# Sigmoid attention and a token/channel mixer on one core: the first group's attention and token mixing in another order

## The chip, the core and the metric

The kernel runs on one core of a Trainium2 chip. Its engines are TensorE (PE; its weight loads are shown as PEld), VectorE (DVE), ScalarE (ACT), GpSimd (POOL) and SyncE (SP). POOL issues the loads from HBM, SP the transposing copies and the stores. The metric is the device time of one execution in microseconds (us), lower is better.

## The reference

For 8 batches, 12 heads, 448 tokens and 64 elements a head, with float32 in HBM:

```python
scores = scale * q @ k.T - log(S)
attn = sigmoid(scores)
x = (attn @ v), heads side by side          # (8, 448, 768)
h = max(x.T @ w_tok1, 0) @ w_tok2           # mixes tokens: 448 -> 256 -> 448
u = x + h.T
out = u + max(u @ w_ch1, 0) @ w_ch2         # mixes channels: 768 -> 1536 -> 768
```

## The kernel before, in words

Matrices are float16 in SBUF, sums float32 in PSUM. Two batches make a group, so there are four groups of 128 rows by 7 token blocks (`J`). A group has six head pairs (`NP`), and a pair has seven score rounds. The order of the instructions on each engine is the order of the program text: nothing is rescheduled.

The steps, with their lines: `load` (L79) brings k, q and v of a pair through POOL. `turn` (L100) transposes k and q of a pair, for the first eight pairs with TensorE (14 small matmuls each, `tk` and `tq`) and a copy out of PSUM, later with a rearranging copy on VectorE and a transposing copy on SP. `scores` (L142) does four matmuls into two banks of PSUM and one sigmoid on ScalarE. `values` (L165) does 28 matmuls over the seven rounds of a pair and copies the result to `xT`, on VectorE for the first group and on ScalarE for the others. `back` (L187) transposes it into `x_nat`. `tok1` (L209) and `tok2` (L226) mix the tokens, with a maximum and a sum after them; the sum is kept as float32 (`u`) and as float16 (`u16`). `uturn` (L293) transposes u16 into `uT` for the channel mixing. `ch1` (L323) and `ch2` (L339) mix the channels, with a maximum and a sum on VectorE.

PSUM has eight banks. Six make three double buffers (`pair_bank`, L63), which scores, values, tok1 and most of tok2 take in turn. Two are single buffers (`bank`, L66), for the transposes, narrow tok2, ch1 and ch2. A matmul into a buffer waits until the engine that read the buffer's last content is done.

`first_attention` (L377) does the first group's attention alone, with no channel mixing to fill gaps. Its `extra` list hangs work behind rounds: the turns of k and q apart, back, and token mixing in three column thirds of 256. Two thirds run inside the attention: tok1 as two stretches of 14 matmuls, then for each of the seven token blocks a tok2, a sum, a cast, two transposes and a copy. The last third follows after the last values (`tok2_late`, L259, which writes u16 first and u afterwards). Before it stands the turn of the second pair of the next group, with ScalarE copying.

`phase` (L427) then does the channel mixing of a group. Between its units, ch1 in 12 steps for four token blocks and 12 for three, then ch2 in 14, stand the next group's score rounds in "visits" of three. A visit may also hold the values of a pair. Each unit has a planned cost, and visits are spread evenly over these costs: 15 visits. After that the next group's tok1, tok2 and uturn stand between ch2 units. The last group has a phase with no attention in it.

The lines that set the visits:

```python
order = [(i, j) for i in range(NP) for j in range(J)]
visits = [order[n : n + 3] for n in range(0, len(order), 3)] + [[]]
for i in range(NP):
    visits[(J * i + J - 1) // 3 + 1].insert(2, (i, None))
step = sum(t for t, _ in units[:n_att]) / len(visits)
```

Of the kernel before, what the change touches and what calls it, by code (L numbers as in the profile page):

```python
# [9 lines left out]
FP16 = mybir.dt.float16  # L10
# [9 lines left out]
def kernel(  # L20
# [26 lines left out]
    JA = 4  # L47
    att_scale = 1.0 / math.sqrt(E)
# [30 lines left out]
    def load(n):  # L79
        g, i = divmod(n, NP)  # L80
        for what, src in (("k", k), ("q", q), ("v", v)):
            t = pa.tile(
                [128, 2, J, E],
                FP16,
                tag="v" if what == "v" else "kq",
                bufs=7 if what == "v" else 8,
                name=f"{what}_{g}_{i}",
            )
            for b in range(2):
                nc.gpsimd.dma_start(  # L90
                    out=t[64 * b : 64 * b + 64, :, :, :],
                    in_=src[2 * g + b, 2 * i : 2 * i + 2].rearrange(
                        "h (p j) e -> p h j e", j=J
                    ),
                )
            heads[(n, what)] = t
# [3 lines left out]
    def turn(n, whats=("k", "q"), eng=nc.vector):  # L100
# [3 lines left out]
        for what in whats:  # L104
# [21 lines left out]
            if eng is nc.vector:  # L126
                eng.tensor_copy(out=t[:, :, :, :], in_=ps[:, :, :, :])  # L127
            else:
                eng.activation(out=t[:, :, :, :], in_=ps[:, :, :, :], func=COPYF)  # L129
        if "q" in whats:  # L130
            load_to(n + 3)

    class Group:
# [31 lines left out]
        def values(self, i):  # L165
# [16 lines left out]
            if self.first:  # L182
                nc.vector.tensor_copy(out=dst, in_=src)
            else:
                nc.scalar.activation(out=dst, in_=src, func=COPYF)
# [23 lines left out]
        def tok1(self, tcb, c0, c1, eng):  # L209
            ps = pair_bank(f"k1_{self.g}_{tcb}_{c0}")  # L210
            for j in range(J):
                for b in range(2):
                    nc.tensor.matmul(  # L213
                        out=ps[:, b, 0 : c1 - c0],
                        lhsT=w_tok1_t[64 * b : 64 * b + 64, j, 128 * tcb : 128 * tcb + 128],
                        rhs=self.x_nat[64 * b : 64 * b + 64, j, c0:c1],
                        start=(j == 0),
                        stop=(j == J - 1),
                    )
            dst, src = self.h1T[:, :, tcb, c0:c1], ps[:, :, 0 : c1 - c0]  # L220
            if eng is nc.vector:
                eng.tensor_scalar(out=dst, in0=src, scalar1=0.0, scalar2=None, op0=MAX)
            else:
                eng.activation(out=dst, in_=src, func=RELU)  # L224

        def tok2(self, j, c0, c1, eng):  # L226
            u, u16 = self.us[j], self.u16s[j]
            if c1 - c0 > 512:
                ps = pair_bank(f"yn_{self.g}_{j}_{c0}")
                w = (c1 - c0) // 2  # L230
                dst = [ps[:, 0, 0:w], ps[:, 1, 0:w]]
                y = ps[:, :, 0:w]
            else:
                w = c1 - c0
                ps = bank(f"yn_{self.g}_{j}_{c0}", [128, w])
                dst = [ps[:, :]]
                y = ps.rearrange("p (n w) -> p n w", n=1)
            for m, d in enumerate(dst):
                for tcb in range(2):
                    for b in range(2):  # L240
                        nc.tensor.matmul(  # L241
                            out=d[64 * b : 64 * b + 64, :],
                            lhsT=w_tok2_n[:, tcb, j, :],
                            rhs=self.h1T[:, b, tcb, c0 + w * m : c0 + w * m + w],
                            start=(tcb == 0),
                            stop=(tcb == 1),
                        )
            nc.vector.tensor_tensor(
                out=u[:, c0:c1].rearrange("p (n w) -> p n w", w=w),
                in0=self.x_nat[:, j, c0:c1].rearrange("p (n w) -> p n w", w=w),  # L250
                in1=y,
                op=ADD,
            )
            if eng is nc.scalar:
                eng.activation(out=u16[:, c0:c1], in_=u[:, c0:c1], func=COPYF)
            else:
                eng.tensor_copy(out=u16[:, c0:c1], in_=u[:, c0:c1])

        def tok2_late(self, js, c0, c1):  # L259

            w = c1 - c0
            name = f"yl_{self.g}_{js[0]}"
            ps = pair_bank(name) if len(js) > 1 else bank(name, [128, 1, w])
            for m, j in enumerate(js):
                for tcb in range(2):
                    for b in range(2):
                        nc.tensor.matmul(
                            out=ps[64 * b : 64 * b + 64, m, 0:w],
                            lhsT=w_tok2_n[:, tcb, j, :],
                            rhs=self.h1T[:, b, tcb, c0:c1],  # L270
                            start=(tcb == 0),
                            stop=(tcb == 1),
                        )
            for m, j in enumerate(js):
                nc.vector.tensor_tensor(
                    out=self.u16s[j][:, c0:c1],
                    in0=self.x_nat[:, j, c0:c1],
# [294 lines left out]
```

## Time and profile before

| what | value |
|---|---|
| median of three runs | 385.68 us (384.07 to 385.81) |
| the profiled execution's own time | 384.07 us |
| its span, first to last instruction | 382.3 us |
| TensorE busy | 360.2 us, 94% of the span |
| VectorE busy | 169.7 us, 44% |
| ScalarE busy | 174.2 us, 46% |
| GpSimd busy | 93.1 us, 24% |
| share of the chain that ended last: PE, DVE, ACT | 89%, 4%, 3% |
| granted TensorE clock | 0.999 |

The page gives an engine's busy time as an average over the whole span. A busy PE there is one that has a matmul in flight, so that it can be full and still lose time where shapes change. The timeline gives for each group of instructions the start, the duration, the engine, the line, the operation and its tiles (written <- read), the shape and the number of instructions; in brackets stands the idle time before it and what ended it. Tiles are named after their step: `qk_g_i_j` a score round, `xa` values, `xb` back, `k_` tok1, `yn` and `yl` tok2, `ut` the transposes of u, and `c_0_3_0` is a ch1 (four blocks) of the first group. The name of a weight tile shows digits left out (`w_tok_t`).

### The profile page before, as it was taken

The numbers are of one execution on the slowest core, as the hardware profiler recorded it, in microseconds if no ns is written. First come the engines' busy times: TensorE is split into PE (matmuls) and PEld (weight loads), VectorE is DVE, ScalarE is ACT, GpSimd is POOL, SyncE is SP. The second block draws the span as 40 slices with busy tenths as digits, with TensorE's granted clock in tenths as the row PEclk, the third lists the DMA queues.
The fourth block names the chain that finished last, engine by engine and source line by source line (L and its number), as shares of the span: only waits on it lengthen the run. The fifth ranks groups of instructions, "written<-read, shape, count | busy, mean of one in ns | idle before, by whom it ended". The sixth has DMA issues, their size and how long they took to land.

```text
span 382.3 us, 8078 instructions
## 1 busy us (share of the span) xinstructions
PE 360.2 (94%) x3404; PEld 189.4 (50%) x3404; DVE 169.7 (44%) x312; ACT 174.2 (46%) x208; POOL 93.1 (24%) x159
## 2 busy tenths in 40 slices
PE   2888987999999999999999999999999999999995
PEld 1444545444555555444555555445555555456663
DVE  1257685553332139544432149444412158555221
ACT  1895752568776510467766410568676210000000
POOL 9888181645154000055153000000000000000000
PEclk9999999999999999999999999999999999999999
DMA  7999999999999936399999927333422327100232
GB/s 102 188 185 172 203 177 201 162 163 146 146 174 134 224 132 155 89 140 123 162 171 172 214 99 165 87 73 74 89 69 74 91 83 158 47 0 0 84 123 84
DMA packets 92372, 49.07 MB, mean 128 GB/s; under 512 B 66096, under 2 KB 88624, under 8 KB 92336
## 3 DMA queue, kind: packets, MB, share of 16 engines
q0 software_dynamic: 25104, 21.93, 40.9%
q1 hardware_dynamic: 67232, 26.62, 36.8%
q8 instruction: 27, 0.44, 0.5%
q14 instruction: 9, 0.07, 0.1%
HBM read 43.84 MB, written 11.01 MB: 143 GB/s over the span
## 4 chain that ended last, share of the span: by engine, by line
PE 89%; DVE 4%; ACT 3%; DMA 1%; issue 1%; POOL 1%; POOLq 0%; ACTq 0%
DMA q_0_78<-in_q_dram 1%; PE c_2_3_1_4494 L343 1%; PE c_2_3_0_4448 L343 1%; PE c_2_2_0_4350 L343 1%; PE c_2_0_1_4232 L343 1%; PE c_1_3_1_3406 L343 1%; PE c_1_3_0_3360 L343 1%; PE c_1_2_0_3262 L343 1%; PE c_1_1_0_3163 L343 1%; PE c_0_3_0_2211 L343 1%; PE c_0_2_1_2148 L343 1%; PE c_0_2_0_2113 L343 1%; PE c_0_1_0_2014 L343 1%; PE c_2_6_1_4697 L343 1%; PE c_2_6_0_4671 L343 1%
## 5 line engine op out<-in xcount | busy, mean ns | idle before, releaser
L326 PEld LDWEIGHTS <-w_ch_t 128*128 128x128 f16 x576 | 53.9, 98 | 58.8 <-issue 12.1
L343 PEld LDWEIGHTS <-h2aT_2475 128*128 128x128 f16 x168 | 15.5, 98 | 13.1 <-issue 3.6
L343 PEld LDWEIGHTS <-h2aT_3624 128*128 128x128 f16 x168 | 15.5, 98 | 13.1 <-issue 3.6
L343 PEld LDWEIGHTS <-h2aT_1316 128*128 128x128 f16 x168 | 15.5, 98 | 13.1 <-issue 3.6
L343 PEld LDWEIGHTS <-h2aT_4712 128*128 128x128 f16 x168 | 16.4, 98 | 10.9
L241 PEld LDWEIGHTS <-w_tok_n 128*64 128x64 f16 x224 | 11.6, 109 | 11.2 <-issue 6.9
L213 PEld LDWEIGHTS <-w_tok_t 64*128 64x128 f16 x252 | 11.5, 94 | 8.8 <-issue 3.0
L90 POOL DMA_DIRECT2D k_0_2644<-in_k_dram x2 | 1.2, 604 | 37.0 <-DVE qp_2535 L110 37.0
L157 ACT ACTIVATE attn_0_0_2494<-qk_0_0_2493 128x896 f16<-128x896 f32 x1 | 0.9, 917 | 17.4 <-PE qk_0_0_2493 L150 17.4
L157 ACT ACTIVATE attn_0_0_3643<-qk_0_0_3642 128x896 f16<-128x896 f32 x1 | 0.9, 917 | 17.4 <-PE qk_0_0_3642 L150 17.4
L121 PE MATMUL tk_133<-ident,k_0_75 128*64 128x128 f16 x14 | 1.0, 312 | 5.2 <-DMA k_0_75<-in_k_dram 5.2
L157 ACT ACTIVATE attn_0_0_167<-qk_0_0_166 128x896 f16<-128x896 f32 x1 | 0.9, 917 | 8.2 <-PE qk_0_0_166 L150 8.2
L127 DVE COPY kT_132<-tk_133 128x896 f16<-128x896 f16 x1 | 0.6, 625 | 6.2 <-PE tk_133 L121 6.2
L121 PEld LDWEIGHTS <-k_0_75 128*64 128x64 f16 x14 | 0.7, 166 | 5.2 <-DMA k_0_75<-in_k_dram 5.2
L90 POOL DMA_DIRECT2D k_3_1923<-in_k_dram x2 | 1.2, 604 | 8.3 <-DVE kp_1804 L110 8.3
L90 POOL DMA_DIRECT2D k_3_3072<-in_k_dram x2 | 1.2, 602 | 8.3 <-DVE kp_2953 L110 8.3
L224 ACT ACTIVATE h1T_2195<-k_1_0_384_2286 128x768 f16<-128x768 f32 x1 | 0.8, 811 | 4.4 <-PE k_1_0_384_2286 L213 4.4
L224 ACT ACTIVATE h1T_4432<-k_3_0_384_4523 128x768 f16<-128x768 f32 x1 | 0.8, 811 | 4.4 <-PE k_3_0_384_4523 L213 4.4
L224 ACT ACTIVATE h1T_3344<-k_2_0_384_3435 128x768 f16<-128x768 f32 x1 | 0.8, 810 | 4.4 <-PE k_2_0_384_3435 L213 4.4
L90 POOL DMA_DIRECT2D k_2_860<-in_k_dram x2 | 1.2, 591 | 6.4 <-PE xb_3_883 L196 3.4
L90 POOL DMA_DIRECT2D k_4_1217<-in_k_dram x2 | 1.2, 590 | 6.4 <-DMA w_ch_t<-in_moe_w_ch_dram 6.4
L129 ACT ACTIVATE kT_1174<-tk_1175 128x896 f16<-128x896 f16 x1 | 0.9, 917 | 3.9 <-PE tk_1175 L121 3.9
(1246 smaller groups left out, 931.2 us busy)
## 6 DMA issues: line engine op xcount, KB each, us to landing
w_ch_t<-in_moe_w_ch_dram POOLq DMA_DIRECT2D x6, 768.0 KB, 12.6
w_tok_t<-in_moe_w_tok_dram POOLq DMA_DIRECT2D x2, 224.0 KB, 6.0
out_dram<-u_0_118 SPq DMA_DIRECT2D x1, 384.0 KB, 8.0
out_dram<-u_1_120 SPq DMA_DIRECT2D x1, 384.0 KB, 6.3
out_dram<-u_2_122 SPq DMA_DIRECT2D x1, 384.0 KB, 4.2
out_dram<-u_3_124 SPq DMA_DIRECT2D x1, 384.0 KB, 2.3
out_dram<-u_4_126 SPq DMA_DIRECT2D x1, 384.0 KB, 3.4
out_dram<-u_5_128 SPq DMA_DIRECT2D x1, 384.0 KB, 2.8
```

Of the source, the lines that this page charges most:

```text
L90: nc.gpsimd.dma_start(out=t[64 * b : 64 * b + 64, :, :, :], in_=src[2 * g + b, 2 * i : 2 * i + 2].rearrange("h (p j) e -> p h j e", j=J),)
L121: nc.tensor.transpose(out=ps[64 * h : 64 * h + 64, j, :, :], in_=raw[:, h, j, :], identity=ident[:, :],)
L127: eng.tensor_copy(out=t[:, :, :, :], in_=ps[:, :, :, :])
L129: eng.activation(out=t[:, :, :, :], in_=ps[:, :, :, :], func=COPYF)
L157: nc.scalar.activation(out=at[:, :, :], in_=ps[:, :, 0:S], func=SIGMOID, bias=att_bias, scale=att_scale,)
L213: nc.tensor.matmul(out=ps[:, b, 0 : c1 - c0], lhsT=w_tok1_t[64 * b : 64 * b + 64, j, 128 * tcb : 128 * tcb + 128], rhs=self.x_nat[64 * b : ...
L224: eng.activation(out=dst, in_=src, func=RELU)
L241: nc.tensor.matmul(out=d[64 * b : 64 * b + 64, :], lhsT=w_tok2_n[:, tcb, j, :], rhs=self.h1T[:, b, tcb, c0 + w * m : c0 + w * m + w], star ...
L326: nc.tensor.matmul(out=ps[:, :, :], lhsT=w_ch1_t[:, db, 128 * cb : 128 * cb + 128], rhs=self.uT[:, db, j0:j1, :], start=(db == 0), stop=(d ...
L343: nc.tensor.matmul(out=ps[:, :], lhsT=self.h2aT[:, cb, j, :], rhs=w_ch2_t[:, cb, c], start=(cb == 0), stop=(cb == NCB - 1),)
```

## The change

The first group's attention is written anew, and some helpers with it. Part by part:

- Loads: v of the first two pairs is loaded behind k and q of both. `turn` always does k and q together and always copies on VectorE.
- Order in a pair i of `first_attention`: two score rounds, the turn of pair i+1, a round, the values of pair i-1, two rounds, back of pair i-1, two rounds, tok1 of pair i-1. Before, the turn of k stood after round 1, that of q after round 3, back after round 5, and tok1 only in pairs 2 and 4.
- tok1 of the first group goes by head pair: 128 columns, both halves of the 256 hidden tokens in one double buffer, 28 matmuls of 128 columns, one maximum on VectorE of 4 x 128.
- tok2 goes by column half (384 columns) in a double buffer. The first half of blocks 0, 1 and 2 runs inside pairs 4 and 5, that of 3 to 6 after the last values. The second half runs late; in a late tok2 of two blocks the second block gets x_nat by an identity matmul into PSUM, so that ScalarE can copy the sum out with no second operand.
- The last values of the first group are copied by ScalarE.
- uturn of two blocks and a half at a time: six transposes and a copy.
- The second half of tok2 of blocks 4 to 6, the transposes of these blocks and the turn of the second pair of the next group stand in the first phase as units of their own, between the first five ch1.
- Visits: the list of rounds with the values counted as rounds (after round 2 of the next pair) is cut in threes, 16 visits, and one more holds the last values. In the first phase the plan starts 6 us late (`ATT_LATE`).

tok1 and tok2 of the other groups have the same matmuls and copies as before.

```diff
+    ATT_LATE = 6.0
...
     def load(n):
...
+        for what, src in (("k", k), ("q", q), ("v", v)):
+            if what == "v" and n < 2:
+                continue
+            load_one(n, what, src)
+        if n == 1:
+            load_one(0, "v", v)
+            load_one(1, "v", v)
...
-            if self.first:
+            if self.first and i < NP - 1:
                 nc.vector.tensor_copy(out=dst, in_=src)
...
+        def tok1(self, c0, c1, tcbs=(0, 1)):
+            w = c1 - c0
+            ps = pair_bank(f"k1_{self.g}_{tcbs[0]}_{c0}")
+            for m, tcb in enumerate(tcbs):
+                for j in range(J):
+                    for b in range(2):
+                        nc.tensor.matmul(
+                            out=ps[:, b, w * m : w * m + w],
...
+        def tok2(self, js, h0=0, h1=2, late=False):
+            ps = pair_bank(f"yn_{self.g}_{js[0]}_{h0}")
+            parts = [(j, half) for j in js for half in range(h0, h1)]
+            for m, (j, half) in enumerate(parts):
+                by_array = late and m == 1
+                if by_array:
+                    nc.tensor.matmul(
+                        out=ps[:, m, 0:DH],
+                        lhsT=ident[:, :],
+                        rhs=self.x_nat[:, j, DH * half : DH * half + DH],
+                        start=True,
+                        stop=False,
+                    )
...
+                def add(dst, x=x, y=y, by_array=late and m == 1):
+                    if by_array:
+                        nc.scalar.activation(out=dst, in_=y, func=COPYF)
+                    else:
+                        nc.vector.tensor_tensor(out=dst, in0=x, in1=y, op=ADD)
+                if late:
+                    add(u16)
+                    steps.append(lambda add=add, u=u: add(u))
+                else:
+                    add(u)
+                    nc.vector.tensor_copy(out=u16, in_=u)
...
     def first_attention(grp):
...
+        early = {(4, 5): (0,), (5, 1): (1,), (5, 5): (2,)}
+        for i in range(NP):
+            for j in range(J):
+                grp.scores(i, j)
+                if j == (1 if i > 0 else 3):
+                    turn(i + 1)
+                elif j == 2 and i > 0:
+                    grp.values(i - 1)
+                elif j == 4 and i > 0:
+                    grp.back(i - 1)
+                elif j == 6 and i > 0:
+                    grp.tok1(128 * i - 128, 128 * i)
+                if (i, j) in early:
+                    grp.tok2(early[(i, j)], 0, 1)
+                if (i, j) == (2, 5):
+                    load_ch1()
+                if (i, j) == (3, 3):
+                    permute_tok2()
+                if (i, j) == (5, 2):
+                    load_ch2()
         grp.values(NP - 1)
+        grp.tok2((3, 4), 0, 1)
         grp.back(NP - 1)
+        grp.uturn((0, 1), 0, 1, nc.vector)
+        grp.tok1(D - 128, D)
+        grp.uturn((2, 3), 0, 1, nc.vector)
+        late = [grp.tok2((0, 1), 1, 2, True), grp.tok2((2, 3), 1, 2, True)]
+        grp.uturn((0, 1), 1, 2, nc.vector)
+        grp.uturn((2, 3), 1, 2)
+        grp.tok2((5, 6), 0, 1)
+        for f in late:
+            f()
...
         for cb in range(NCB):
+            add(1.3, grp.ch1, cb, 0, JA, nc.scalar if grp.first and cb < 3 else nc.vector)
+            if grp.first and cb == 0:
+                add(0.7, grp.tok2, (4, 5), 1, 2)
+            if grp.first and cb == 1:
+                add(0.4, grp.tok2, (6,), 1, 2)
+                add(0.4, grp.uturn, (4, 5), 0, 1)
+            if grp.first and cb == 2:
+                add(0.4, grp.uturn, (4, 5), 1, 2)
+            if grp.first and cb == 3:
+                add(0.4, grp.uturn, (6,))
+            if grp.first and cb == 4:
+                add(1.0, turn, NP + 1)
...
-        order = [(i, j) for i in range(NP) for j in range(J)]
-        visits = [order[n : n + 3] for n in range(0, len(order), 3)] + [[]]
-        for i in range(NP):
-            visits[(J * i + J - 1) // 3 + 1].insert(2, (i, None))
-        step = sum(t for t, _ in units[:n_att]) / len(visits)
+        visits = [rounds[n : n + 3] for n in range(0, len(rounds), 3)]
+        visits.append([(NP - 1, None)])
+        at = -ATT_LATE if grp.first else 0.0
+        step = (at + sum(t for t, _ in units[:n_att])) / len(visits)
```

## The prediction

> **What bounds the kernel now.** I read four views, in this order: the page's 40 slices, the table of stretches, the timeline by engine, the order of the instructions. The slices first (a slice is 9.6 us):
>
> ```profile
> PE   2888987999999999999999999999999999999995
> DVE  1257685553332139544432149444412158555221
> ACT  1895752568776510467766410568676210000000
> ```
>
> TensorE (PE) is short of full only in the first seven or so slices and in the last. The stretches say it in microseconds (columns: stretch, length, busy time of PE, weight loads, VectorE, ScalarE, GpSimd with their counts, clock, DMA share, GB/s):
>
> ```profile
> 0.00:20.00 20.00, 10.61 (x164) 6.18 (x164) 4.42 (x7) 10.70 (x13) 17.06 (x34) 1.00 0.99 147
> 20.00:40.00 20.00, 17.16 (x271) 9.86 (x267) 14.06 (x31) 15.09 (x18) 16.13 (x26) 1.00 1.19 179
> 40.00:60.00 20.00, 17.05 (x276) 9.67 (x273) 14.42 (x32) 11.92 (x14) 9.39 (x15) 1.00 1.19 189
> 60.00:80.00 20.00, 17.39 (x173) 9.41 (x173) 10.65 (x27) 10.51 (x15) 9.68 (x17) 1.00 1.19 180
> 80.00:100.00 20.00, 20.00 (x197) 9.35 (x198) 8.58 (x17) 14.30 (x17) 8.72 (x15) 1.00 1.35 148
> ```
>
> So there are two regimes. From about 73 us PE is never free: there a change costs the PE time that it adds, and hidden work on other engines is worth nothing. In the first attention (9.6 to 68.9 us) PE, VectorE and ScalarE wait for each other by turns, and only there can order win. PE's timeline there:
>
> ```profile
> 26.15 0.56 PE L196 MATMUL xb_1_509<-ident,xT_1_457 128*128 128x128 f16 x7
> 26.64 0.38 PE L150 MATMUL qk_2_6_519<-qT_334,kT_272 64*64 64x448 f16 x4
> 27.52 0.94 PE L213 MATMUL k_0_0_0_526<-x_nat_115,w_tok_t 64*128 64x256 f16 x14 [0.50 <-ACT attn_2_5_503 L157]
> 28.39 0.38 PE L150 MATMUL qk_3_0_542<-qT_466,kT_404 64*64 64x448 f16 x4
> ...
> 58.47 0.36 PE L171 MATMUL xa_5_1124<-attn_5_6_1107,v_5_357 64*64 64x448 f16 x4
> 58.76 0.29 PE L306 MATMUL ut_4_2_1155<-ident,u_0_4_127 128*128 128x128 f16 x2
> ...
> 68.92 1.46 PE L326 MATMUL c_0_0_0_1318<-uT_117,w_ch_t 128*128 128x512 f16 x6 [0.35 <-ACT uT_117 L316]
> ...
> 74.55 1.46 PE L326 MATMUL c_0_3_0_1373<-uT_117,w_ch_t 128*128 128x512 f16 x6
> 75.94 0.38 PE L150 MATMUL qk_0_3_1398<-qT_1024,kT_945 64*64 64x448 f16 x4
> 76.16 0.36 PE L150 MATMUL qk_0_4_1405<-qT_1024,kT_945 64*64 64x448 f16 x4
> 76.34 0.36 PE L150 MATMUL qk_0_5_1412<-qT_1024,kT_945 64*64 64x448 f16 x4
> 76.64 1.47 PE L326 MATMUL c_0_4_0_1419<-uT_117,w_ch_t 128*128 128x512 f16 x6
> 77.94 1.46 PE L326 MATMUL c_0_5_0_1427<-uT_117,w_ch_t 128*128 128x512 f16 x6
> ```
>
> The first number is the start; the difference of two starts is what a piece costs PE. The marks to beat: the last values end at 58.76, c_0_0 starts at 68.92, c_0_5 at 77.94.
>
> **Prices**, all as such differences. A score round 0.32 before another shape, about 0.20 among its like; its sigmoid starts 0.44 to 0.50 after it, takes 0.92, and frees the PSUM buffer 0.05 later. A turn of k or q 0.51. Values 1.32; their copy starts 1.57 after them and takes 1.09. A back 0.49; its copy starts 0.60 after it, takes 0.62. Eight tok2 matmuls of 384 columns 0.67 to 0.75. From VectorE's timeline:
>
> ```profile
> 24.69 1.09 DVE L183 CAST xT_1_457<-xa_1_428 128x896 f16<-128x896 f32 x1 [1.32 <-PE xa_1_428 L171]
> 26.75 0.62 DVE L199 COPY x_nat_115<-xb_1_509 128x896 f16<-128x896 f16 x1 [0.44 <-PE xb_1_509 L196]
> ...
> 31.05 0.41 DVE L248 TENSOR_TENSOR u_0_118<-x_nat_115,yn_0_0_589 128x256 f32<-128x256 f16 x1
> 31.50 0.29 DVE L257 CAST u_0_0_119<-u_0_118 128x256 f16<-128x256 f32 x1
> ```
>
> A sum and cast of 384 columns, between these and the 768-column ones of the later groups (0.95 and 0.56), are 0.55 + 0.36.
>
> **Part 1, tok1 by head pair.** Six stretches of 28 matmuls of 128 columns take the place of six of 14 matmuls of 256 columns (0.87 each). Columns are the same, twice the weight loads; the trace has no such stretch. Below: 0.87, if loads stay hidden (a loss of nothing). Above: a back pays 0.49 for 7 matmuls of 128 columns with full weights, 0.070 each, so 28 x 0.070 = 1.96. Between: the turns of k and q together are 28 matmuls of 128 columns on half-array tiles in 1.02, with two changes of shape. tok1 runs in half-array tiles too (64 rows), so that row is nearest; less one change of shape (0.09) I take **0.93**. The Trainium skill, "TensorE: Matmul & The Clock Gate", Back-to-back issue gap, speaks against the change: it gives about 81 ns per matmul of 128 columns for a stream that reloads weights. By it a stretch is 2.27, and the total 8 us more than mine; the trace's 36 to 70 ns for the same width do not bear it out, so my sum does without it.
>
> **Part 2, the cycle of a head pair.** In the new order PE goes: score, score, turn k and q, score, values, two scores, back, two scores, tok1. Three PSUM buffers are shared by scores, values, tok1 and tok2. From one qk_i_0 to the next: 0.57 (first score, then the wait for the sigmoid two rounds earlier), 0.32, turn 1.02, 0.22, then values to back 1.57 + 1.09 + 0.04 = 2.70 (two scores inside, about 0.9 idle), back to tok1 0.60 + 0.62 + 0.05 = 1.27 (two scores inside, 0.4 idle), tok1 0.93: **7.03 us**. ScalarE's seven sigmoids (5.6) fit inside, so it is not the bound. The start is unchanged (k_0 and q_0 keep their places in POOL's queue; v_0 and v_1 move behind k_1 and q_1 and are needed only after 17 us). Going round by round with these prices, ScalarE's 0.80 per sigmoid sets the pace until qk_1_2 and I get qk_2_0 at 21.9 (now 20.88: the first tok1 comes before it). Then pairs 2 and 3 end at 36.1 (0.1 for permute_tok2 on VectorE). In pairs 4 and 5 a tok2 takes a buffer, so tok1 gets that of qk_i_5, whose sigmoid ends 1.95 after back, not 1.27: 7.71, and 8.06 with the second tok2 (0.35). Values of pair 5 start at 51.9 and end at 53.2: **5.5 us earlier** than 58.76.
>
> **Part 3, the tail up to c_0_0.** A new wait: the copy of x_nat for pair 5 stands on VectorE behind two sums and casts of tok2(3,4), which start 0.93 after the values' end and take 1.75. Behind the copy wait tok1, tok2 and every transpose. So tok1 starts at +3.35, its maximum on VectorE ends at +5.07, two late tok2 with the identity matmuls (each 0.70 + 0.16 + two changes of shape, 1.0) end at +7.1, sums (ScalarE beside VectorE) to +7.85, two transposes and tok2(5,6) to +8.95. c_0_0 starts at 62.15, not 68.92: **6.8 earlier**.
>
> **Part 4, what was put off.** Up to c_0_5 PE must still do five ch1 (6.5), tok2(4,5) and (6) (1.05), three lots of transposes (1.08), three scores (0.7) and the turn of pair 1 of the next group (1.02): 10.35. Waits: tok2(4,5) reuses the buffer of the first late tok2, and VectorE frees it only after copies, two sums and casts and the late sum, at +11.45, where PE is there at +10.25: 1.2. The two PSUM banks of ch1 and the transposes now alternate, so ch1 waits for the maximum just before: 0.45 twice, 0.25 and 0.1 (the same kind of wait shows 0.46 today before c_0_1). In all 12.8, so c_0_5 starts at 74.95. Today it starts at 77.94, but with three more scores done (0.70 + 0.09): 77.15. **2.2 us are left.**
>
> **Part 5, the phases.** The visits' list changes for groups 1 to 3: rounds, values among them, are cut in threes, 17 visits, not 15. A visit costs PE a change of shape twice: c_0_3 to qk_0_3 is 1.39 where c_0_4 to c_0_5 is 1.30, and three scores take 0.70 where three times 0.19 is 0.56. That is 0.23 a visit, two more in each of three phases: **+1.4**. In the first phase qk_2_0 to qk_2_2 come one ch1 after the visit before, 2.1 us, while three sigmoids need 2.96: the third score waits 0.4. DMAs: POOL's loads keep their number; the ch2 weights go behind the loads of one pair and are needed only near 109 us; SP's transposes interleave otherwise (values before the turn), and k has some 10 us between turn and use. Nothing.
>
> **Sum.** -2.2 + 1.4 + 0.4 = -0.4 us. Against the profiled execution (span 382.3, its time 384.07) that is 383.7. That execution was the fastest of three; their median is 385.68, and the same step from it gives **385.3**, my forecast: no change that can be told (0.5%, 1.9 us, is about what a measurement tells).
>
> **Rivals.**
> - *Slower: tok1 is bound by its weight loads.* For it: twice the loads, 0.070 each in a back. Against: 0.036 in a turn. The place is the six k_0 stretches, all on PE's path; at 1.96 each they cost 6 x 1.03 = 6.2, so 391.5 from the median, 389.9 from the profiled run. It decides from 1.25 a stretch (6 x 0.32 = 1.9). Chance 0.25.
> - *It does not do what it says.* Three PSUM buffers, not the order of the text, limit how far scores run ahead; if VectorE and ScalarE answer as late as today, c_0_5 comes no earlier and only the visits and the wait stay: +1.8, 387.5. For it: today's waits on ScalarE for a buffer (0.4 each). Against: VectorE has 28 instructions fewer. Chance 0.17, about half of it beyond 0.5%.
> - *Faster: the tail's new waits are not there.* x_nat of pair 5 (1.4 later than its data), tok2(4,5) (1.2) and two of the ch1 waits (0.7) sum to 3.3, if VectorE's queue runs ahead of what I charge: -3.7, 382.0. Against: the queue's order is fixed. Chance 0.18.
>
> The forecast has 0.40. Faster 0.18; the same 0.40 + 0.09 = 0.49; slower 0.25 + 0.08 = 0.33. The range is 382.0 to 390.0: it takes in the first end of the fast case and tok1 up to 1.7 a stretch. The forecast's own range is 383.5 to 387.5.
>
> **What would show it.** tok1 stretches of 0.93 (part 1); qk_i_0 seven us apart for pairs 2 and 3 and the last values near 53 (part 2); c_0_0 near 62 with x_nat of pair 5 late on VectorE (part 3); an idle stretch of about 1 us before tok2(4,5) (part 4); PE full from 75 us on, and each later phase 0.5 longer (part 5). Wrong it would be if tok1 takes over 1.25, if loads of k or q are late for a pair (today the longest such wait is 0.24), or if PE shows waits in the phases.

## The result, and the profile after

The changed kernel takes **390.18 us** (median of six executions, 388.57 to 392.34) against 385.34 us for the kernel before (six executions beside it, 384.07 to 385.93): ratio 1.013, 95% interval [1.009, 1.017]. It is slower by more than a measurement is uncertain. The profiled execution has 388.96 us and a span of 387.2 us, 4.9 us more than before.

Two rows of the 40 slices of the changed kernel, which answer to those of the prediction (a slice is 9.7 us):

```profile
PE   2888779895999999999999999999999999999995
PEclk9999999998999999999999999999999999999999
```

The 5 in the tenth slice of PE's row and the 8 in the clock's row are new; both fall between 87 and 97 us, where the prediction had PE "never free". The table of stretches shows the same (columns as before; the clock is the last but two):

```profile
60.00:80.00 20.00, 18.41 (x162) 8.49 (x161) 11.27 (x23) 11.71 (x17) 7.46 (x14) 1.00 1.08 171
80.00:100.00 20.00, 15.97 (x144) 7.28 (x143) 5.35 (x11) 10.88 (x14) 5.88 (x10) 0.91 1.40 129
```

From 60 to 80 us PE is now busier (18.41 against 17.39), as meant. From 80 to 100 us it loses 4 us of busy time (15.97 against 20.00), and the mean clock is 0.91. PE's timeline names the place:

```profile
21.02 0.96 PE L221 MATMUL k_0_0_0_390<-x_nat_115,w_tok_t 64*128 64x128 f16 x28 [0.31 <-DVE x_nat_115 L204]
21.91 0.38 PE L155 MATMUL qk_2_0_420<-qT_289,kT_272 64*64 64x448 f16 x4
...
52.45 0.84 PE L254 MATMUL yn_3_0_1127<-h1T_116,w_tok_n 128*64 128x384 f16 x8
...
62.05 1.47 PE L318 MATMUL c_0_0_0_1254<-uT_117,w_ch_t 128*128 128x512 f16 x6
...
74.35 1.46 PE L318 MATMUL c_0_5_0_1402<-uT_117,w_ch_t 128*128 128x512 f16 x6 [0.33 <-DVE kT_1359 L135]
...
91.93 0.38 PE L155 MATMUL qk_2_0_1601<-qT_1414,kT_1410 64*64 64x448 f16 x4 [4.03 <-DMA qT_1414<-qp_1415]
...
92.62 2.10 PE L318 MATMUL c_0_0_4_1622<-uT_117,w_ch_t 128*128 128x384 f16 x6
94.52 1.89 PE L318 MATMUL c_0_1_4_1630<-uT_117,w_ch_t 128*128 128x384 f16 x6
96.24 1.14 PE L318 MATMUL c_0_2_4_1638<-uT_117,w_ch_t 128*128 128x384 f16 x6
```

Read the starts. The first attention did what it should: values end at 52.45 (58.76 before), c_0_0 starts at 62.05 (68.92), c_0_5 at 74.35 (77.15 for the same work). Then PE waits 4.03 us at 91.93 for qT of pair 8 (the third pair of the second group), and the next two ch1 take 1.90 and 1.72 from start to start, where the kernel before has 0.98 to 0.99 for such a ch1. That is 1.66 us more in a time in which the granted clock is down: 0.67 from 91.93 to 94.00, 0.55 from there to 96.24, and 1.00 again behind it. The same score in the kernel before, with no wait in front of it:

```profile
89.13 0.36 PE L150 MATMUL qk_2_0_1580<-qT_1385,kT_1381 64*64 64x448 f16 x4
```

The whole difference, by marks of the two PE timelines:

| stretch | before | after | difference |
|---|---|---|---|
| start to c_0_5 (same work) | 77.15 | 74.35 | -2.8 |
| c_0_5 to c_1_0 | 77.18 | 83.67 | +6.5 |
| c_1_0 to c_2_0 | 84.65 | 85.38 | +0.7 |
| c_2_0 to c_3_0 | 84.32 | 84.78 | +0.5 |
| c_3_0 to the end | 59.0 | 59.0 | 0.0 |

(A ratio in this document leaves out executions over 1.5% above the fastest of the same kernel; since every such execution that was profiled holds a wait behind a late landing, the median and range of all executions stand beside each ratio.)

Of the 6.5 us, 4.03 are the wait, 1.66 the slow ch1, some 0.46 two more visits (what they cost in a later phase), and 0.35 are not assigned.

Why is qT late? Three views of the changed kernel. GpSimd's timeline (POOL; k_5, q_5, v_5 are the loads of pair 11, k_0, q_0, v_0 those of pair 12):

```profile
65.57 0.60 POOL L99 DMA_DIRECT2D v_4_1399<-in_v_dram  x1 [4.77 <-DMA w_ch_t<-in_moe_w_ch_dram]
73.94 1.18 POOL L99 DMA_DIRECT2D k_5_1418<-in_k_dram  x2 [7.77 <-PE tk_1360 L130]
75.10 1.21 POOL L99 DMA_DIRECT2D q_5_1421<-in_q_dram  x2
76.27 1.29 POOL L99 DMA_DIRECT2D v_5_1424<-in_v_dram  x2
77.53 1.22 POOL L99 DMA_DIRECT2D k_0_1540<-in_k_dram  x2
78.69 1.24 POOL L99 DMA_DIRECT2D q_0_1543<-in_q_dram  x2
79.86 1.26 POOL L99 DMA_DIRECT2D v_0_1546<-in_v_dram  x2
```

The transposes on SP's queue, and then what the list of DMA issues says of the second (the last number is the time from issue to landing):

```profile
76.93 1.33 SPq L122 DMA_TRANSPOSE kT_1410<-kp_1411  x1
78.31 1.96 SPq L122 DMA_TRANSPOSE qT_1414<-qp_1415  x1
```

```profile
qT_1414<-qp_1415 SPq DMA_TRANSPOSE x1, 13.5
```

The same two views of the kernel before, whose transposes were issued at 77.13 and 78.52:

```profile
72.63 1.23 POOL L90 DMA_DIRECT2D k_5_1389<-in_k_dram  x2
73.79 1.25 POOL L90 DMA_DIRECT2D q_5_1392<-in_q_dram  x2
74.95 1.27 POOL L90 DMA_DIRECT2D v_5_1395<-in_v_dram  x2
77.34 1.19 POOL L90 DMA_DIRECT2D k_0_1495<-in_k_dram  x2 [1.11 <-DVE qp_1386 L110]
79.21 1.19 POOL L90 DMA_DIRECT2D q_0_1498<-in_q_dram  x2 [0.69 <-DVE h2aT_1316 L335]
80.38 1.22 POOL L90 DMA_DIRECT2D v_0_1501<-in_v_dram  x2
```

```profile
qT_1385<-qp_1386 SPq DMA_TRANSPOSE x1, 7.0
```

The transposes are issued within 0.2 us of each other in the two kernels, but qT lands after 7.0 us before and 13.5 us after. What differs is their company. The k load of pair 11 takes over the buffer (`kq`, eight of them, four pairs) that pair 7's k leaves, and the turn of pair 7 was put off into the first phase (`tk_1360`). So POOL stands for 7.77 us, and then twelve loads of 112 KB (two in a row of this view) go out without a break, right around the transposes. The kernel before issues the same twelve loads, but those of pair 11 end 2.3 us ahead of qT's transpose (here 0.75), and there are pauses behind them. The difference in timing is small; the experiments have to show whether it is enough.

### The profile page after: what moved, and what is told of

The parts are those of the page before. It is cut to its first block, busy times and chain, and to the rows that moved or that the text cites. A ratio compares the mean times of both kernels' runs of the same rounds, so it can differ in the third digit from the quotient of the medians.

```text
span 387.2 us, 8171 instructions
## 1 busy us (share of the span) xinstructions
PE 360.1 (93%) x3462; PEld 189.3 (49%) x3462; DVE 164.9 (43%) x284; ACT 177.2 (46%) x211; POOL 93.2 (24%) x159
## 4 chain that ended last, share of the span: by engine, by line
PE 85%; DMA 5%; DVE 4%; ACT 2%; issue 1%; SPq 1%; POOL 1%; POOLq 0%; ACTq 0%
DMA qT_1536<-qp_1537 3%; DMA x_nat_2489<-xT_5_3354 2%; SPq L122 1%; DMA q_0_78<-in_q_dram 1%; PE c_2_3_0_4461 L335 1%; PE c_2_2_1_4398 L335 1%; PE c_2_2_0_4370 L335 1%; PE c_2_1_1_4309 L335 1%; PE c_2_1_0_4274 L335 1%; PE c_1_4_1_3480 L335 1%; PE c_1_2_0_3282 L335 1%; PE c_1_1_1_3204 L335 1%; PE c_0_4_1_2331 L335 1%; PE c_0_3_0_2224 L335 1%; PE c_0_2_1_2161 L335 1%
## 5 line engine op out<-in xcount | busy, mean ns | idle before, releaser
L221 PEld LDWEIGHTS <-w_tok_t 64*128 64x128 f16 x336 | 12.9, 94 | 11.8 <-issue 4.9
L99 POOL DMA_DIRECT2D k_0_2681<-in_k_dram x2 | 1.2, 604 | 36.5 <-DVE qp_2548 L119 36.5
L233 ACT ACTIVATE h1T_3357<-k_2_0_384_3448 128x768 f16<-128x768 f32 x1 | 0.8, 811 | 5.0 <-PE k_2_0_384_3448 L221 5.0
L99 POOL DMA_DIRECT2D k_3_3117<-in_k_dram x2 | 1.2, 604 | 7.9 <-DVE qp_2970 L119 7.9
L99 POOL DMA_DIRECT2D k_5_1418<-in_k_dram x2 | 1.2, 596 | 7.8 <-PE tk_1360 L130 7.8
L233 ACT ACTIVATE h1T_4445<-k_3_0_384_4536 128x768 f16<-128x768 f32 x1 | 0.8, 811 | 4.4 <-PE k_3_0_384_4536 L221 4.4
```

The lines of the kernel that those rows point to most:

```text
L99: nc.gpsimd.dma_start(out=t[64 * b : 64 * b + 64, :, :, :], in_=src[2 * g + b, 2 * i : 2 * i + 2].rearrange("h (p j) e -> p h j e", j=J),)
L221: nc.tensor.matmul(out=ps[:, b, w * m : w * m + w], lhsT=w_tok1_t[64 * b : 64 * b + 64, j, 128 * tcb : 128 * tcb + 128], rhs=self.x_nat[64 ...
L233: nc.scalar.activation(out=dst, in_=src, func=RELU)
```

## The experiments

Theory first held: this **buffer gate** makes the late loads, and the loads make qT late. Rivals: the new **visits** (pair 8 needed 1.2 us earlier, at 87.90 and not 89.13; another order on SP's queue); the **weights** of ch2, issued 3.5 us later on POOL's queue. Each run was timed with the kernel before on the same chip.

| run | median, range (us) | ratio to before, 95% interval |
|---|---|---|
| turn of pair 7 early | 386.12 (384.67 to 396.03) | 1.003 [0.999, 1.006] |
| 12 buffers | 397.76 (396.05 to 399.24) | 1.031 [1.027, 1.036] |
| 15 visits | 388.27 (384.19 to 390.59) | 1.006 [1.002, 1.009] |
| before, 17 visits | 388.16 (384.92 to 389.88) | 1.004 [1.000, 1.008] |
| weights first | 387.76 (384.20 to 390.53) | 1.004 [1.001, 1.007] |
| turn of pair 8 early | 385.64 (383.35 to 391.97) | 0.999 [0.995, 1.002] |
| loads of pair 12 held | 390.76 (389.43 to 394.16) | 1.015 [1.011, 1.018] |
| turn of pair 8 early, 15 visits | 385.96 (381.81 to 388.98) | 0.993 [0.990, 0.997] |
| lead of a pair | 393.39 (388.65 to 399.51) | 1.018 [1.013, 1.023] |
| lead, 15 visits | 398.65 (392.31 to 405.62) | 1.026 [1.020, 1.032] |
| before, lead | 401.58 (388.67 to 408.82) | 1.009 [1.004, 1.015] |
| lead, 15 visits, tail | 397.55 (392.51 to 405.57) | 1.022 [1.017, 1.027] |
| turn of pair 7 in the tail | 387.06 (382.15 to 391.50) | 0.999 [0.995, 1.003] |
| the same, 6 buffers | 383.48 (381.92 to 384.73) | 0.993 [0.990, 0.996] |
| turn in the tail, 15 visits | 383.99 (380.85 to 388.29) | 0.992 [0.988, 0.995] |
| **turn in the tail, 6 buffers, 15 visits** | **380.56** (380.04 to 382.72) | **0.987** [0.983, 0.991] |
| before, 6 buffers | 385.44 (384.28 to 388.54) | 1.002 [0.999, 1.005] |
| 6 buffers alone | 390.37 (387.35 to 391.02) | 1.012 [1.009, 1.015] |

In the timelines of these runs a name carries no numbers, and like neighbours are one row.

**Turn of pair 7 early.**

```diff
         grp.tok2((5, 6), 0, 1)
+        turn(NP + 1)
...
-            if grp.first and cb == 4:
-                add(1.0, turn, NP + 1)
```

> Theory (buffer gate): the turn of pair 7 (second pair of the next group), put into the first phase, holds the buffer that the k load of pair 11 reuses, so that POOL stands idle until 73.9 us and then issues twelve loads in a row, beside SP's transposes for pair 8. With this turn back at the end of the first attention the loads of pair 11 go out from about 66 us, qT of pair 8 lands in about 7 us and not 13.5, and the 4.0 us wait before qk_2_0 goes, with the 1.7 us of slow ch1 behind it: 390.2 - 5.7 = 384.5 us, 384 to 385.5. Rival (visits): the new list of visits asks for qk_2_0 1.3 us earlier and orders SP's queue otherwise; then the wait stays and the time is 389.5 to 390.5. Rival (weights): the ch2 weights, 3.4 us later on POOL's queue, push all later loads back; then too most of the wait stays, 388 or more.

In the profiled execution the wait for qT of pair 8 went, and with it the slow ch1: its landing took 7.9 us. But the time is 386.1 and not 384.5: in the tail VectorE copies kT and qT ahead of what c_0_0 needs, as PE's timeline shows.

```profile
66.18 1.46 PE L318 MATMUL c<-uT,w_ch_t 128*128 128x512 f16 x6 [1.73 <-DVE kT L135]
```

c_0_0 starts 4.1 later than in the changed kernel. So this run doesn't price the first attention. Nor does it prove the gate: the wait is gone with the turn elsewhere, but turn 8 came 3.9 us later too, and so met fewer loads.

**12 buffers.**

```diff
-            bufs=7 if what == "v" else 8,
+            bufs=7 if what == "v" else 12,
```

> Only the number of k and q load buffers changes, 8 to 12, and no instruction moves. Theory (buffer gate): POOL no longer waits for the turn of pair 7; pairs 11 and 12 are loaded from 66 us on, ahead of SP's transposes, and the wait before qk_2_0 goes with the slow ch1 behind it: 384.5 us, about as with the turn moved. If what matters is the bytes in flight and not when POOL is let go, the wait only moves: 387 to 389. Rivals (visits, weights): 389 to 390.5.

The theory in its first form falls here. POOL's 7.77 us of waiting for `tk` are gone, but the wait before qk_2_0 is not, and at the end of the phase comes another:

```profile
92.54 0.76 PE L155 MATMUL qk<-qT,kT 64*64 64x448 f16 x12 [4.12 <-DMA qT<-qp]
...
148.14 2.10 PE L221 MATMUL k<-x_nat,w_tok_t 64*128 64x384 f16 x12 [7.43 <-DMA x_nat<-xT]
```

Without the gate most loads of pair 11 still went out at 74.2 to 77.5, because they stood behind the ch2 weights, and those of pairs 12 and 13 right behind them (77.5 to 86.9, with a few gaps). With the loads let go earlier qT took 13.6 us. So POOL's wait is not what does the damage; what is left to suspect is loads beside transposes.

**15 visits, and the kernel before with 17.** The one edit puts the earlier lines that set the visits into the changed kernel (shown), the other puts the new ones into the kernel before (the same diff reversed):

```diff
-        visits = [rounds[n : n + 3] for n in range(0, len(rounds), 3)]
-        visits.append([(NP - 1, None)])
+        order = [(i, j) for i in range(NP) for j in range(J)]
+        visits = [order[n : n + 3] for n in range(0, len(order), 3)] + [[]]
+        for i in range(NP):
+            visits[(J * i + J - 1) // 3 + 1].insert(2, (i, None))
```

> The changed kernel with the earlier list of 15 visits. Theory (buffer gate): qT of pair 8 still lands near 92 us; asked for about 1.3 us later, it makes PE wait some 2.7 us; two visits less in each of three phases save 1.4 (0.46 a phase, as measured between the two traces): 390.2 - 1.3 - 1.4 = 387.5 us, 386.5 to 388.5. Rival (visits): no wait is left and the clock stays up: 390.2 - 5.7 - 1.4 = 383.1 us.

> The kernel before with the new list of 17 visits and nothing else. Theory (buffer gate): POOL's loads stay as before, qT of pair 8 lands near 85.5 us and is asked for near 88, so no wait of over 0.3 us: only the visits' price of 0.46 to 0.6 a phase, 385.3 + 1.4 to 1.8 = 386.7 to 387.1 us. Rival (visits): a wait of some us appears before qk_2_0, 389 to 391 us.

Both speak against the rival: a wait is left with 15 visits, and none comes with 17. The times agree less well with the theory than they seem to (388.3 where 387.5 was expected; 1.004 is 1.6 us where 1.4 to 1.8 was, though the median is 2.5 up). The profiled execution with 15 visits is the fastest of its twelve, 384.19, and why the median is 4 us above it no trace shows. In it a wait of 2.75 is left, and the ch1 behind it run at full speed: two of them, of three token blocks each, in 2.12, as where nothing waits:

```profile
90.98 0.38 PE L155 MATMUL qk<-qT,kT 64*64 64x448 f16 x4 [2.75 <-DMA qT<-qp]
91.29 2.12 PE L318 MATMUL c<-uT,w_ch_t 128*128 128x384 f16 x12
```

The kernel before with 17 visits has no wait for k or q in its profiled execution (385.01, one of its three fastest). The phases from c_1_0 on, where PE has no wait in them, take 84.31 to 84.32 with 15 visits and 84.77 to 84.78 with 17, in all these kernels: 0.46 for two visits, 0.23 each. So the visits cost what was foretold and make no wait by themselves in these two executions. Their earlier need adds little to one that is there: with 15 visits pair 8 is wanted at 88.23 and not 87.90, 0.33 of the 1.28 us by which the wait is shorter; the rest is a landing after 12.1 us and not 13.5.

**Weights first.**

```diff
+                if (i, j) == (5, 0):
+                    load_ch2()
                 if j == (1 if i > 0 else 3):
...
-                if (i, j) == (5, 2):
-                    load_ch2()
```

> The changed kernel with the ch2 weights one step ahead on GpSimd's queue, before the loads of pair 9, as in the kernel before. Theory now (late loads): in the runs so far qT of pair 8 lands in 7.0 to 8.2 us where the last load of pair 11 was issued 2.3 us or more ahead of it, and in 12.1 to 13.6 us where it was issued 0.7 to 1.4 us ahead; either the buffer held by the turn of pair 7 or the later weights is enough to make these loads late. Then this edit alone changes nothing, since the buffer still holds GpSimd until about 74 us: wait of about 4 us before qk_2_0, 389.5 to 390.5 us. If the weights are what matters, the wait goes: 384.5 to 386 us.

Neither forecast: 387.8. The gate held POOL until 75.4, the twelve loads went out in a row, yet qT of pair 8 landed in 9.7 us, just in time; in its place a later pair waits 2.39, and the two ch1 behind that wait take 3.78 and not 2.12, at a granted clock of 0.57.

```profile
100.49 0.38 PE L155 MATMUL qk<-qT,kT 64*64 64x448 f16 x4 [2.39 <-DMA qT<-qp]
```

The weights alone aren't the cause; how long a transpose takes in such company differs.

**Turn of pair 8 early**, without and with 15 visits:

```diff
-        if j == 3 and not grp.first:
+        if j == 3 and not grp.first and (grp.g, i) != (1, 0):
...
                 add(0.4, grp.uturn, (4, 5), 1, 2)
+                add(0.0, turn, NP + 2)
```

> The turn of pair 8 alone is moved from the second visit to the third ch1, some 10 us earlier; everything else, the loads' burst too, stays. Theory (late loads meet the transposes of pair 8): these transposes are now done before the burst, no wait at qk_2_0 and no slow ch1: 390.2 - 4.0 - 1.7 = 384.5 us, 384 to 386 (up to 1 us may come back as a wait for pair 9). Rival (SP's own queue is slow, whatever the loads do): pair 9's transposes inherit the delay, 387 to 390 us.

> The turn of pair 8 at the third ch1 and the earlier list of 15 visits. Theory: no wait in the first phase, 0.46 us less in each of three phases: 384.5 - 1.4 = 383.1 us, from the marks of the traces 74.4 + 77.2 + 84.3 + 84.3 + 59.0 = 379.2 span, 381 us for an execution as good as the profiled ones; about 0.99 of the kernel before. Rival: a later pair waits instead, 385 us or more.

The best executions (383.35, and 381.81) are near the expected times, but about half of them are 3 to 9 us longer, the two profiled ones among them: there pair 8 has no wait, and a later one waits 4.38 and 3.99 us. So in these two the loss was moved to the next transposes that meet loads, as one rival had it; that the other long executions lost their time in the same way is likely, but no trace shows it.

**Loads of pair 12 held.**

```diff
+        if n == 2 * NP:
+            nc.vector.memset(t[0:128, 0, 0, 0:1], 0.0)
         for b in range(2):
             nc.gpsimd.dma_start(
```

> Only the six loads of pair 12, which go out right beside the transposes of pair 8 in every kernel so far, are held back behind VectorE's copies for the turn of pair 9 (one column of each buffer is written by VectorE before its load). Theory in its wide form (any loads beside the transposes slow them): qT of pair 8 lands in 6 to 9 us, no wait at qk_2_0, 384.5 to 385.5 us, or a wait at a later pair if the held loads then collide with its transposes. In its narrow form (the loads of pair 11 are what is in the way): qT still needs over 11 us, wait of 2 to 4 us, 388 to 390 us.

This shows the contention by itself. GpSimd's timeline, and the two transposes of pair 8 (issued at 76.80 and 78.17, as in the changed kernel):

```profile
76.13 1.29 POOL L101 DMA_DIRECT2D v<-in_v_dram  x2
83.16 1.19 POOL L101 DMA_DIRECT2D k<-in_k_dram  x2 [5.74 <-DVE v L99]
```

```profile
kT<-kp SPq DMA_TRANSPOSE x1, 5.5
qT<-qp SPq DMA_TRANSPOSE x1, 5.0
```

The loads of pair 11 are where they were; only those of pair 12 are gone, and qT lands in 5.0 us, not 13.5. The wide form holds: the loads issued beside and behind a transpose slow it. The Trainium skill, "DMA: Bandwidth & Descriptors", Issuing engines are not separate DMA queues, says that DMAs issued by SP and by GpSimd run on the same 16 DMA engines and interleave; these two landings agree. The held loads go out from 83.2 on, and those of the next pairs behind them up to 99.4, around the transposes of pairs 9 and 10, which land in up to 10.5 and 11.8 us; PE waits 0.56 and 3.14 there. The time doesn't change (390.8): in all the loads are as many.

**Lead of a pair**: every transposing turn seven rounds earlier, pair 8 at the third ch1, a fourth buffer for the turned k and q; then with 15 visits, in the kernel before, and with a shorter tail.

```diff
-            t = pa.tile([128, J, 2, P], FP16, tag=f"{what}T", bufs=3, name=f"{what}T_{n}")
+            t = pa.tile([128, J, 2, P], FP16, tag=f"{what}T", bufs=4, name=f"{what}T_{n}")
...
-            turn(grp.g * NP + i + 2)
+            turn(grp.g * NP + i + 3)
...
+                add(0.0, turn, NP + 2)
```

> The changed kernel with every transposing turn one head pair (some 11 us) earlier, the turn of pair 8 at the third ch1, and a fourth buffer for the turned k and q. No transpose or load is left out, so they still collide on the DMA queues; only the time until the need grows. Theory (the loss is a late landing and the slow clock behind it, and not PE's own work): no wait over 0.5 us for k or q in any phase; from the marks 74.4 to c_0_5, 77.7 for the rest of the first phase, 84.8 twice, 59.0: span 380.6, time 382.4, that is 0.994 of the kernel before. Rival (the transposes can't keep pace at all, the queue falls behind by more with each pair): waits stay, 386 us or more.

> The same with the earlier list of 15 visits: 0.46 us less in each of three phases, 74.4 + 77.2 + 84.3 + 84.3 + 59.0 = 379.2 span, 381.0 us, 0.990 of the kernel before, and an execution varies less than without the lead (where 381.8 to 389.0 was seen), since no landing is near its need. Rival: 385 us or more, as above.

> The kernel before with the same lead: turns one pair earlier, pair 8 at the second ch1, a fourth buffer. Its profiled execution had no wait for k or q, so the span stays 382.3 and the best times at 383.5 to 384; where other executions (up to 389) were late landings they go, so that the median falls to about 384. Against the last run it then shows what the first attention alone is worth: 3 us (2.8 by the marks). If the lead itself costs (VectorE's copies in the tail), 385 to 386.

> The run with lead and 15 visits, and in the tail the sums of tok2(3,4) written first as float16 alone, the second block's by ScalarE after an identity matmul, with the float32 sums behind the copy of x_nat of pair 5. The copy of x_nat then waits for one sum of 0.55 us and not for 1.75 of sums and casts; PE's wait of 1.37 before tok1 of pair 5 shrinks by about 1.0, the identity matmul costs 0.25: 0.7 us less than the run with 15 visits, 380.3 us. Rival (VectorE's queue is as long in the end and the float32 sums delay tok1's maximum behind it): no gain or 0.3 us slower.

All four missed, by 11 to 18 us at the median, the kernel before among them; the profiled executions are among the longest of each. In these PE no longer waits over 0.5 us for k or q, but another engine now pays. From the kernel before with the lead, its list of waits from 60 to 200 us (us in total, times, longest) and PE's timeline:

```profile
DVE qp L110 <- DMA kT<-kp: 21.5, 4, 11.4
```

```profile
121.99 2.08 PE L326 MATMUL c<-uT,w_ch_t 128*128 128x384 f16 x6 [5.69 <-DVE h2aT L335]
```

VectorE copies k and q into one of three `perm` buffers before a transpose, and waits until the transpose that last read that buffer has landed. Behind that copy in VectorE's queue stand the maxima of ch1, and PE waits for those. With 15 visits and with the shorter tail PE also waits 7.33 and 6.82 us for x_nat at the end of the first phase, again for a landing. A longer lead against a late DMA only helps if nothing else waits for the same DMA. Whether the shorter tail is worth its 0.7 us can't be read under this loss and stays open.

**Turn of pair 7 in the tail, 8 and 6 buffers, 17 and 15 visits.** The turn goes where the kernel before has it, with ScalarE copying (`turn` takes `whats` and `eng` again, as before the change):

```diff
-            bufs=7 if what == "v" else 8,
+            bufs=7 if what == "v" else 6,
...
         grp.tok2((3, 4), 0, 1)
+        turn(NP + 1, "k", nc.scalar)
         grp.back(NP - 1)
+        turn(NP + 1, "q", nc.scalar)
...
-            if grp.first and cb == 4:
-                add(1.0, turn, NP + 1)
```

> The turn of pair 7 goes back to where the kernel before has it, around back of pair 5, with ScalarE copying, so that it fills waits of the tail (1.4 to 1.6 us each) and not the first phase. c_0_5 then starts about 1.0 earlier, near 73.3, and the buffer is free by 56 us. Without waits: 73.3 + 77.7 + 84.8 + 84.8 + 59.0 = 379.6 span, 381.4 us. Theory (loads beside the transposes): GpSimd's queue is behind by the weights, so that the last load of pair 11 goes out near 76 and qT of pair 8 near 77: landing in 12 us or more, a wait of 2 to 4 with slow ch1 behind it, 384 to 387 us. Rival (the buffer alone): no wait, 381 to 383 us.

> The same with 6 buffers for k and q in place of 8: loads run one pair less ahead, those of pair 11 are held until VectorE's copies for the turn of pair 8. Theory: at the transposes of pair 8 only these six loads are beside them, as the six of pair 12 are in the kernel before, nothing older is in the way: qT lands in 7 to 8.5 us, no wait; the early loads are bound by bytes and not by buffers, so the first attention stays: 381.4 us, 381 to 383, 0.99 of the kernel before. Rival (less run-ahead only makes the loads themselves late): waits for v, k or q in the first attention or in the phases, 386 us or more.

> Turn of pair 7 in the tail, 8 buffers, the earlier list of 15 visits: asked for 1.3 us later, and 1.4 us less of visits. Theory: landing as in the run with the turn in the tail, wait 1 to 3 us: 382 to 384.5 us. Without a wait: 73.3 + 77.2 + 84.3 + 84.3 + 59.0 = 378.1 span, 379.9 us.

> Turn of pair 7 in the tail, 6 buffers, 15 visits. Theory: no wait for k or q: 378.1 span, 379.9 us, 0.987 of the kernel before, and executions closer together than with 8 buffers. Rival: loads late, 385 us or more.

With 8 buffers the time is at the end of the expected range (387.1), but its executions lie from 382 to 391. The profiled one (385.25) waits only 1.28 us for a transpose; that a late landing makes the long ones fits the rest, but isn't shown for this kernel. With 6 buffers they stand together. The best kernel, with 15 visits, takes 380.56, 1.3% less than the kernel before and 2.5% less than the changed one. Its slices, GpSimd's timeline and the transposes of pair 8, issued at 77.37 and 78.74:

```profile
PE   2878879999999999999999999999999999999995
...
PEclk9999999999999999999999999999999999999999
```

```profile
65.85 0.60 POOL L99 DMA_DIRECT2D v<-in_v_dram  x1 [4.19 <-DMA w_ch_t<-in_moe_w_ch_dram]
77.58 1.18 POOL L99 DMA_DIRECT2D k<-in_k_dram  x2 [11.13 <-DVE qp L119]
78.74 1.21 POOL L99 DMA_DIRECT2D q<-in_q_dram  x2
79.91 1.23 POOL L99 DMA_DIRECT2D v<-in_v_dram  x2
84.35 1.20 POOL L99 DMA_DIRECT2D k<-in_k_dram  x2 [3.22 <-DVE qp L119]
```

```profile
kT<-kp SPq DMA_TRANSPOSE x1, 5.9
qT<-qp SPq DMA_TRANSPOSE x1, 7.8
```

POOL waits even longer (11.13 us), and that is good: it waits for the copies of pair 8, so that only six loads go out beside these transposes, and the next six come 3.22 us after them. c_0_5 starts at 73.49 and c_1_0 at 150.64 (154.33 before). In the profiled execution no wait above 0.5 us is left on PE after 62 us.

**What the buffers do alone.** The last two runs have `bufs` 6 and no other edit, in the kernel before and in the changed one.

> The kernel before with 6 buffers for k and q in place of 8, nothing else. Theory (what run-ahead of the loads costs is late transposes, in some executions of the kernel before too, which range from 383.4 to 389): the median falls to about 384, 0.995 of the kernel before, and the executions stand closer together. Against the run with the turn in the tail, 6 buffers and 15 visits (380.6) the first attention is then worth 3 to 3.5 us, as the marks say (c_0_5 at 73.5 against 77.15). Rival (6 buffers starve the first attention): 386.5 us or more.

> The changed kernel with 6 buffers and nothing else: the turn of pair 7 stays in the first phase. Then the loads of pair 10 wait for it until 74 us and those of pair 11 for the turn of pair 8: twelve loads in a row beside the transposes of pair 8, as in the changed kernel. Theory: qT needs 11 us or more, a wait of 2 to 4 us, 387 to 390 us. Rival (the number of buffers alone heals it): no wait, 383.5 to 385 us.

Six buffers bring the kernel before nothing (1.002; the closer executions that I expected did not come), and the changed kernel nothing either: the turn of pair 7 then holds the loads of pair 10 (15.24 us of waiting on POOL), and twelve loads again meet the transposes, of which that of qT takes 14.0 us.

```profile
92.69 0.93 PE L155 MATMUL qk<-qT,kT 64*64 64x448 f16 x12 [4.56 <-DMA qT<-qp]
93.54 4.57 PE L318 MATMUL c<-uT,w_ch_t 128*128 128x384 f16 x18
```

(Eighteen matmuls of ch1 take 3.10 at full clock.) So the place of the turn decides at 6 buffers (383.5 in the tail, 390.4 in the phase; some 1.0 of it because the turn now fills waits of the tail, c_0_5 at 73.55 and not 74.57), and the buffers decide how steadily the gain comes. The first attention, with what moved along with it, is worth 4.2 us between the profiled spans of the two kernels with 6 buffers and 15 visits (382.5 and 378.3), or 3.7 by the start of c_1_0 against the kernel before.

Stays open: why in one execution a transpose takes 8 us and in another 12 in like company. In four kernels qT of pair 8 took 12.1 to 14.0 us where the loads of the older pair had ended only 0.7 to 1.4 us before its issue and six more went out beside it, and in seven 6.8 to 8.2 where the older ones had ended 2.3 us or more ahead; but 9.7 with the weights first (0.7), and 12.0 with the turn in the tail and 15 visits (2.7). In the six kernels with pair 8 turned early it took 12.8 to 14.9; in five of them POOL was still waiting for a ch2 weight load at that time, so that weights were the company there.

## Why the prediction was wrong

- **Part 1, right.** A tok1 stretch takes 0.89 (21.02 to 21.91), foretold 0.93. The slower rival, weight loads that show, is dead: 28 matmuls in 0.89 are 0.032 each.
- **Part 2, right, the gain a little larger.** From one qk_i_0 to the next 6.81, 7.25 and 7.20 us for pairs 2 to 4 and 7.84 to the last values, where 7.03, 7.03, 7.71 and 8.06 were foretold; the last values end at 52.45, not 53.2.
- **Part 3, right in mechanism, the mark by luck.** tok1 of pair 5 waits 1.37 for x_nat on VectorE, as described, and starts 3.37 behind the values (foretold 3.35). c_0_0 at 62.05, foretold 62.15; but the tail took 9.60 us and not 8.95, and the mark fits only because it began 0.75 earlier.
- **Part 4, right in sum.** c_0_5 at 74.35, foretold 74.95: 2.8 us gained, not 2.2. From c_0_0 it is 12.30, foretold 12.8. The wait of 1.2 before tok2(4,5) did not come. Which buffer it took was read wrongly: it starts at 63.63, as VectorE is done with that of tok2(5,6), and before it reads that of the first late tok2 for the last time, at 63.89. Waits of 0.35, 0.45 and 0.33 before ch1 did come.
- **Part 5, the failed step.** The visits cost 0.23 each, as foretold. But "DMAs: POOL's loads keep their number; ... SP's transposes interleave otherwise ..., and k has some 10 us between turn and use. Nothing." was wrong: worth 4.03 us of waiting and 1.66 us of slow ch1. The lead was right (qT issued at 78.31, wanted at 87.90, some 10 us); the landing, 7.0 us before, got no term of its own, and was 13.5. The step counted the loads but not when they go out. The turn of pair 7 was counted as 1.02 us of PE; that it also holds a buffer for which POOL stands was not followed.
- **Sum.** -0.4 was foretold; measured it is -2.8 + 4.03 + 1.66 + 0.46 (visits) + 0.35 (not assigned) + 0.7 + 0.5 = +4.9. Of the 0.7 of the second phase 0.46 are visits; the rest is what is left of a wait of 0.54 for x_nat, again a landing on SP's queue, since the kernel before loses 0.33 there too (84.65 against 84.32). The third score's wait of 0.4 could not show here, behind the longer one (0.42 with the turn in the tail). The range's upper end, 390.0, came from a rival on PE; no case held a DMA that lands late, though the text named one under what would make it wrong.
- **Rivals.** "It does not do what it says" is dead by the marks. "Faster" was right in one of its three waits, tok2(4,5); that for x_nat and those before ch1 came.

## What to carry to other kernels

When a step is moved, follow not only its instructions but the buffer that it frees: who waits for that buffer, when that queue now bursts, and which transfer with a deadline it then meets. A transfer's lead has to be compared with its landing in company, not with the landing that the old order shows. Load buffers are a brake as well as a supply: here fewer of them, released by the right step, were worth more than more buffers or a longer lead.

## What the runs showed of the hardware

- A transposing copy of a 128x896 f16 tile (qT of pair 8) landed in 5.0 us where the next six loads were held, in 6.8 to 8.2 with six loads of 112 KB beside it (12.0 once), and in 9.7 to 14.0 with twelve in a row around it.
- After 4.03 us without a matmul the next two ch1 took 1.90 and 1.72 us, and the third has its usual duration of 1.14 again; after 4.56 us three ch1 took 4.57 instead of 3.10; after 2.75 us there was no loss. But after 2.39 us (weights first) two ch1 took 3.78 instead of 2.12, and after 1.91 us (lead, 15 visits, tail) 3.79, with a granted clock of 0.5 to 0.6 behind each:

```profile
91.60 3.79 PE L318 MATMUL c<-uT,w_ch_t 128*128 128x384 f16 x12 [1.91 <-DVE h2aT L327]
```

The Trainium skill, "TensorE: Matmul & The Clock Gate", What's actually happening, puts the fall to half clock after an idle window of about 3.4 us, and full clock after as long a busy one. The waits of 4.03, 4.56 and 2.75 us fit that, those of 2.39 and 1.91 don't: the length of a wait alone did not decide here, and what else did isn't shown.

- Twelve k and q buffers in place of eight made the changed kernel slower still, from 1.013 to 1.031 of the kernel before.
